# Other steps for the scales' transposes, the staged w_o rows and the memory updates of a two-layer attention and gated-MLP kernel

## The chip, the cores and the metric

The kernel runs on one core of a Trainium2 chip. The metric is the device time of one execution in microseconds (us). The engines are TensorE (PE: matmul, and PEld: its weight loads), VectorE (DVE), ScalarE (ACT), GpSimd (POOL) and SyncE (SP), whose queue issues the DMAs.

## The reference, cut to what matters

Two kinds of layer alternate twice: x + A(layernorm(x)), then x + B(layernorm(x)). x has 2048 rows of 640. A is attention with 32 heads of 20 columns in four segments of 512 rows. Inside a segment it is causal softmax attention; beside it every head reads a memory M (20 x 20) and z (20) of the segments before, and adds its own keys and values to them:

```python
for s in range(N):
    qs, ks, vs = q[:, :, s], k[:, :, s], v[:, :, s]
    p = _softmax(einsum("bhqd,bhkd->bhqk", qs, ks) * scale + mask)
    a_dot = einsum("bhqk,bhkd->bhqd", p, vs)
    num = einsum("bhld,bhde->bhle", phi(qs), M)
    den = einsum("bhld,bhd->bhl", phi(qs), z)[..., None] + 1e-6
    outs.append(g * num / den + (1.0 - g) * a_dot)
    M = M + einsum("bhld,bhle->bhde", phi(ks), vs)
    z = z + einsum("bhld->bhd", phi(ks))
```

The heads' outputs are multiplied by w_o. B is a gated MLP: z = gelu(x w_in), its second half is normalised and mixed over the 2048 rows by w_sp, multiplied with the first half, and multiplied by w_out.

## The kernel before, in words

Each of the two layers has three phases in the trace: attention (`phase1a`), the w_in products (`phase1b`), and the mixing and w_out products (`phase2`). Nearly all products are made from pairs of 16-bit halves, a high half (`h`) and a low half (`l`, what the high half leaves), after scaling by powers of two, so that an operand is always prepared by a cast on ScalarE and a subtraction on VectorE or GpSimd.

**The calendar of attention.** 64 pairs of heads (four segments, 16 pairs each) pass through a loop over steps t, from -16 up (`run`). Two pairs take five steps. A step emits, in this order: fetches of queries and keys of a later pair (`fetch`, SP), the combination of a finished pair (`combine`, VectorE and GpSimd), the logits by queries of a later pair with the maxima of their rows (`by_queries`, tile `mp`, reduced by VectorE into `mxs`), the logits by keys of the present pair (`by_keys`, tile `es`) with their exponentials (ScalarE, into `P` or `Pb`), in steps t = 5n + 2 the transposed maxima (`maxes`), whatever was posted for this step (`later`), the products of P with the values (`pvs`, tile `pv`, 20 matmuls a head), the casts of P to halves (`cast`: `PH` by ScalarE, `PL` by GpSimd, in four pieces a pair), and then the streams that are spread over the steps: layernorms of later rows, projections to q, k, v (`unit`, `value`) and by w_o (`project`), memory reads (`read`), the background weights (`background`). Work posted into `half` comes between two turns of the streams. The order of TensorE's instructions in this phase is the order in which they are emitted. The other engines' orders are chosen by the framework's scheduler from a timeline that it estimates and from priorities; `issue_after(e)` holds an instruction of e's engine behind e, and `behind(engine)` does that for the maxima and exponentials of the present step (`lead`).

**The bank "ms".** Four things share one PSUM bank (pool `apm`, tag "ms", one buffer): the transposed maxima (`mtp`, L1331, evicted by ScalarE L1333 and VectorE L1335 into `mr`, then four DMAs into the query tile, L1338), the memory update (`mup`, L1203 to L1205, 12 matmuls, evicted by VectorE L1209 into `mst`, to which GpSimd adds the old memory, L1211), the memory reads (`num`, L1175 and L1179, evicted by VectorE L1184 and L1188), and the transposes that find the weights' scales (`wtp`, L60, and `wbc`, L67).

**Updates.** A key projection's eviction (`out`) makes the feature phi(k) in one step's second half and `keys` in the next: ScalarE and VectorE split it (L1147, L1148), a transposing DMA turns it into `pk` (L1151, one buffer), and `update` is posted for the first step at least three ahead whose t mod 5 is in `UPD` and that neither is nor follows a step with a memory read. There are 15 updates a layer. Reads stand in the steps 40 s + (-6, -1, 9, 14, 24) and, for the last group of heads, 29, for segments s = 1 to 3.

**Background, layer 1 only.** Layer 1 finds the scales of w_o, w_in and w_out (`other_scales`: 32 loads into staging tiles and reductions of them, then the two transposes of `pow2_parts`), splits w_o (five rows, `Weight.behind`, L155, L81, L82) and the second half of w_in (ten pieces), and stores the halves (L166). Layer 2 loads the stored halves. The staging rows of w_o are parts of the tile that later holds the halves of w_in.

**The end of the phase.** The last half of the last pair's `PL` is made by VectorE instead of GpSimd (`TAIL`). `phase1b` begins with `load(0)` (L359, from DRAM) and the layernorm of its first row block, emitted under a raised priority, so that they mix with the end of attention; the five w_in row loads of its first half (L129) have a priority raised further, behind the last maxima's DMAs.

## Time and profile before

| | us |
|---|---|
| median of 3 runs | 2235.47 (2233.04 to 2241.97) |
| the profiled execution | 2232.87 |
| its span | 2231.2 |
| attention, layer 1 | about 27 to 603 |
| w_in products, layer 1 | about 603 to 849 |
| mixing and w_out, layer 1 | about 849 to 1133 |
| attention, layer 2 | about 1133 to 1694 |
| w_in products, layer 2 | about 1694 to 1932 |
| mixing and w_out, layer 2 | about 1932 to 2231 |

A view of groups or of waits names the waiting instruction, then the one that released it ("PE mup L1203 <- DVE mr L1335"): the total, the number of times, the longest. In a view of a queue in order of time the first two numbers are start and length, and a bracket gives the engine's idle time just before and what ended it. A view of stretches gives the length, then each engine's busy time with its number of instructions, TensorE's granted clock as a share of full speed, the DMA engines' share and GB/s. Step numbers are counted from the order in which the logits by queries (`mp`, L1249) begin: step 34 of layer 1 begins at 184.65 us, step 50 at 257.16, step 73 at 335.64; in layer 2 they begin at 1300.75, 1359.51 and 1429.37.

### The profile page before, as it was taken

To read this page: it belongs to the slowest core of one execution; us is meant where nothing else is said; L and a number is where in the kernel's file an instruction comes from. 1 tells how busy PE (TensorE), PEld (TensorE's weight loads), DVE (VectorE), ACT (ScalarE), POOL (GpSimd) and SP (SyncE) were. 2 spreads that over 40 slices of the span, in tenths; PEclk is the share of its full clock that TensorE was granted. 3 is DMA by queue.
4 is the path that set the end of the run, shared out by engine and by line. 5 is a ranking of instruction groups with operands and counts; after the bars stand their busy time and mean duration, and the time that the engine had idled before them with its cause. 6 is when DMAs were issued, how large, how long until landed. Compare 5 with 4: busy or idle time off the path is not lost.

```text
span 2231.2 us, 53044 instructions
## 1 busy us (share of the span) xinstructions
PE 2092.0 (94%) x21322; PEld 1264.7 (57%) x21322; DVE 1624.2 (73%) x2889; ACT 1252.3 (56%) x1641; POOL 1404.3 (63%) x1172
## 2 busy tenths in 40 slices
PE   6898788999899999999998999989999999999999
PEld 3554555666555555555554556656675555555555
DVE  8788778788677758888746787787875765676563
ACT  4587688788644433333325887878884433333331
POOL 3387888888645446466513888988895533564660
PEclk9999899999999999999999999999999999999999
DMA  6665556444676686676455356552456345877752
GB/s 185 157 177 141 157 150 188 109 120 126 166 195 188 180 260 191 155 189 175 132 170 129 98 128 166 127 129 75 125 137 152 98 123 175 216 181 177 166 150 83
DMA packets 537703, 342.79 MB, mean 154 GB/s; under 512 B 411600, under 2 KB 463312, under 8 KB 537456
## 3 DMA queue, kind: packets, MB, share of 16 engines
q1 hardware_dynamic: 537456, 339.39, 56.8%
q8 instruction: 167, 2.74, 0.5%
q14 instruction: 80, 0.66, 0.1%
HBM read 159.18 MB, written 92.55 MB: 113 GB/s over the span
## 4 chain that ended last, share of the span: by engine, by line
PE 67%; DVE 14%; ACT 7%; DMA 5%; issue 4%; POOL 2%; SPq 1%; DVEq 0%; ACTq 0%; POOLq 0%
PE zp L412 12%; PE ga L669 12%; PE cyp L705 7%; PE pv L1353 4%; PE qps L1110 3%; PE mp L1249 3%; PE gb L669 3%; PE vps L1051 3%; PE yps L1083 3%; PE gc L669 3%; PE gd L669 3%; DVE mxs L1313 3%; PE kps L1110 2%; PE es L1249 2%; ACT PH L1322 2%
## 5 line engine op out<-in xcount | busy, mean ns | idle before, releaser
L1324 POOL TENSOR_TENSOR PL<-P,PH 128x640 f16<-128x640 f32 x384 | 539.4, 1433 | 91.8 <-PE pv L1353 74.2
L1313 DVE TENSOR_REDUCE mxs<-mp 128x2 f32<-128x1024 f32 (+2 forms) x384 | 320.6, 862 | 135.3 <-PE mp L1240 133.7
L1287 ACT ACTIVATE P<-es,sc 128x1024 f32<-128x1024 f32 (+1 forms) x256 | 271.3, 1060 | 97.0 <-PE es L1240 92.3
L639 POOL TENSOR_TENSOR ts<-ts,wt 128x512 f32<-128x512 f32 x196 | 281.8, 1449 | 11.0
L412 PEld LDWEIGHTS <-th 128*128 128x128 f16 x1920 | 188.0, 98 | 169.3 <-issue 6.6
L1322 ACT CAST PH<-P 128x1280 f16<-128x1280 f32 x192 | 239.6, 1248 | 2.5 <-PE pv L1353 1.0
L669 PEld LDWEIGHTS <-wts 128*128 128x128 f16 x1536 | 150.7, 98 | 134.6 <-issue 6.7
L669 PE MATMUL ga<-zh,wts 128*128 128x432 f16 x768 | 212.0, 348 | 3.9 <-ACT u L736 3.9
L308 POOL TENSOR_TENSOR lnrs<-lnve,mhalf 128x1 f32<-128x1 f32 x96 | 59.7, 629 | 230.0 <-DVE lnve L307 223.7
L1324 POOL TENSOR_TENSOR PL<-Pb,PH 128x640 f16<-128x640 f32 x124 | 176.8, 1454 | 19.8 <-PE pv L1353 18.6
L412 PE MATMUL zp<-wi,th 128*128 128x432 f16 x960 | 181.2, 346 | 3.6 <-ACT z L448 3.6
L1051 PE MATMUL vps<-wvh,xt 128*128 128x320 f16 x640 | 155.5, 309 | 30.3 <-DVE relu L1142 22.1
L639 POOL TENSOR_TENSOR ts<-wt,wt 128x512 f32<-128x512 f16 x28 | 34.4, 1230 | 227.7 <-DMA wt<-wn 227.7
L669 PEld LDWEIGHTS <-wt 128*128 128x128 f16 x1152 | 112.7, 98 | 96.5
L1353 PE MATMUL pv<-vs,PH 128*128 128x41 f16 x2560 | 159.5, 183 | 8.2 <-DVE gm L1374 5.9
L705 PE MATMUL cyp<-wuh,ut 128*128 128x320 f16 (+1 forms) x896 | 163.6, 299 | 2.6 <-DMA ut<-un 1.8
L705 PEld LDWEIGHTS <-ut 128*128 128x128 f16 (+1 forms) x1344 | 131.1, 98 | 57.4 <-DMA ut<-un 3.9
L1249 PEld LDWEIGHTS <-qk 64*128 64x128 f16 (+1 forms) x2048 | 77.6, 94 | 149.4 <-issue 130.9
L1353 PE MATMUL pv<-vs,PL 128*128 128x41 f16 x2560 | 157.2, 182 | 2.2 <-POOL PL L1324 2.2
L412 PE MATMUL zp<-wi1h,th 128*128 128x432 f16 x640 | 149.8, 349 | 1.9 <-DMA th<-xnhl 1.9
L1353 PEld LDWEIGHTS <-PH 128*128 128x128 f16 x2560 | 139.4, 96 | 15.8 <-issue 5.9
L523 DVE SCALAR_TENSOR_TENSOR wn<-wr,wsc,wn 128x512 f16<-128x512 f32 x126 | 92.2, 770 | 75.5 <-ACT wn L522 75.4
(224 smaller groups left out, 5283.3 us busy)
## 6 DMA issues: line engine op xcount, KB each, us to landing
qk<-st SPq DMA_DIRECT2D x256, 120.0 KB
wr<-in_B_w_sp_dram SPq DMA_DIRECT2D x60, 512.0 KB
z<-z SPq DMA_DIRECT2D x32, 432.0 KB
cz<-z SPq DMA_DIRECT2D x32, 432.0 KB
xt<-in_A_x_dram SPq DMA_DIRECT2D x32, 320.0 KB
st<-qhl SPq DMA_DIRECT2D x40, 256.0 KB
st<-khl SPq DMA_DIRECT2D x40, 256.0 KB
x<-x SPq DMA_DIRECT2D x32, 320.0 KB
```

Source lines behind the costliest of these rows:

```text
L412: nc.tensor.matmul(zp[:, n, :FHH], a[:, k, :], b[:, k, c:c + FHH], start=(k == 0 and j == 0), stop=(k == KD - 1 and j == 2))
L639: nc.gpsimd.tensor_tensor(t, a, t if b == "t" else get(b), ALU.add if op == "+" else ALU.subtract)
L669: nc.tensor.matmul(ps, w[:, a, k % 4, :], z[:, k, j, :], start=start and k == 0 and i == 0, stop=k == NP - 1 and i == 2, skip_group_check= ...
L705: nc.tensor.matmul(yp[:, n, :320], a[:kn[k], k, :], b[:kn[k], k, n * 320:(n + 1) * 320], start=(k == 0 and j == 0), stop=(k == KO - 1 and ...
L1051: nc.tensor.matmul(ps, a[:, k, c], b[:, k, n * 320:(n + 1) * 320], start=(i == 0), stop=(i == 14))
L1110: nc.tensor.matmul(ps, a[:, k, c], b[:, k, :], start=(i == 0), stop=(i == 14))
L1249: nc.tensor.matmul(out[:, h, o:o + w], a[r, ac], b[r, bc], start=o == 0, stop=False, skip_group_check=True)
L1287: g.exp = nc.scalar.activation(P, E, AF.Exp, scale=g.esc)
L1313: e = nc.vector.tensor_reduce(mx[:, :, n, j], mp[:, :, o:o + w], AX.X, ALU.max)
L1322: nc.scalar.copy(PH, P[:, h])
L1324: (nc.gpsimd if h == 0 or n < self.N - self.TAIL else nc.vector).tensor_tensor(PL[:, c], P[:, h, c], PH[:, c], ALU.subtract)
L1353: nc.tensor.matmul(pv[:, i, h, :41], x[:, c:c + 128], v[:, j, h0 + h, :], start=(j == 0 and x is PH), stop=(j == i and x is PL), skip_grou ...
```

## The change

Six edits. `load(0)` gets three times the priority offset. `UPD` loses 2, so that no update falls into a step with the transposed maxima; `keys` is put off by a step while an update is still waiting. The last pair's low half on VectorE is posted two steps later. In the background of layer 1 the two transposes of the scales move from steps 39 and 40 to 41 and 45, the five w_o rows are loaded in steps 42 to 44 instead of 45.5 to 47.5 and split from step 47 instead of 48; and every step of the weights' work is also held behind the exponentials of its step on ScalarE.

```diff
@@ phase1b
+        with tc.high_priority(offset=3 * HP2):
+            a = load(0)
         with tc.high_priority(offset=HP2):
-            a = load(0)
             xn = attn_out(0, *a)
@@
-UPD = (2, 3, 4, 0)
+UPD = (3, 4, 0)
@@ Attention.__init__
-        self.mem, self.last, self.stacked = False, -1, -1
+        self.mem, self.last, self.stacked, self.waiting = False, -1, -1, False
@@ Attention.out
         def keys(ph):
+            if self.waiting:
+                self.post(1, lambda: keys(ph))
+                return
+            self.waiting = True
             hl = self.u3.tile([128, 2, L], F16, tag="hl", name="phl")
@@ Attention.update
         assert self.pk_of == (s, m), (self.pk_of, s, m)
+        self.waiting = False
@@ Attention.cast
-        for c in (slice(0, 640), slice(640, 1280))[::-1 if n % 2 and h else 1]:
-            (nc.gpsimd if h == 0 or n < self.N - self.TAIL else nc.vector).tensor_tensor(PL[:, c], P[:, h, c], PH[:, c], ALU.subtract)
+
+        def low(engine):
+            for c in (slice(0, 640), slice(640, 1280))[::-1 if n % 2 and h else 1]:
+                engine.tensor_tensor(PL[:, c], P[:, h, c], PH[:, c], ALU.subtract)
+
+        if h == 0 or n < self.N - self.TAIL:
+            low(nc.gpsimd)
+        else:
+            self.post(2, lambda: low(nc.vector))
@@ Attention.run, background
             if not made:
-                for i, _ in enumerate(other_scales(g, self.place, self.pl1, self.pm, "ms")):
+                scales = other_scales(g, self.place, self.pl1, self.pm, "ms")
+                for i, more in enumerate(scales):
+                    if not more:
+                        break
                     yield 5 + i
-            yield 45
-            yield 45.5
-            for j, (w, width) in enumerate(((g.wo, D), (g.wi[1], FHH))):
-                w.tiles(g.top[j])
...
-                else:
-                    parts = [...]
-                    it = w.behind(lambda _: next(rows), width, KD)
-                    times = [46 + i / 2 for i in range(KD)] + [49 + 1.4 * i for i in range(99)]
-                for i in range(99):
-                    with self.tc.issue_after(self.fetched.ins):
-                        if next(it, it) is it:
-                            break
-                    yield times[i]
+                yield 41
+                next(scales)
+
+            def steps(it, times):
+                for t in times:
+                    with self.tc.issue_after(self.fetched.ins), self.behind(ACT):
                         if next(it, it) is it:
                             break
+                    yield t
+
+            g.wo.tiles(g.top[0])
+            if made:
+                yield 45.5
+                yield from steps(g.wo.load(self.bg, D, "bg"), [46 + 1.4 * i for i in range(99)])
+                g.wi[1].tiles(g.top[1])
+                yield from steps(g.wi[1].load(self.bg, FHH, "bg"), [54 + 1.4 * i for i in range(99)])
+            else:
+                parts = [...]
+                rows = iter([parts[k // 3][:, k % 3] for k in range(KD)])
+                it = g.wo.behind(lambda _: next(rows), D, KD)
+                yield 42
+                yield from steps(it, [42.5, 43, 43.5, 44, 45])
+                next(scales, None)
+                yield 47
+                yield from steps(it, [48.4 + 1.4 * i for i in range(99)])
+                g.wi[1].tiles(g.top[1])
+                yield from steps(g.wi[1].behind(self.place, FHH, 2), [56 + 1.9 * i for i in range(99)])
```

## The prediction

> **What bounds it now.** I read the page first, then the busy time of stretches, then who waited for whom in the stretches where the two layers differ, then single queues in order of time.

> ```profile
> span 2231.2 us, 53044 instructions
> PE 2092.0 (94%) x21322; PEld 1264.7 (57%) x21322; DVE 1624.2 (73%) x2889; ACT 1252.3 (56%) x1641; POOL 1404.3 (63%) x1172
> PE 67%; DVE 14%; ACT 7%; DMA 5%; issue 4%; POOL 2%; SPq 1%; DVEq 0%; ACTq 0%; POOLq 0%
> ```

> TensorE carries the kernel: busy 94%, and two thirds of the chain that ended last. The change takes no matmul away, so it can only win where TensorE waits. The edits lie in the attention phases (about 27 to 603 and 1133 to 1694 us), and there the two layers are a comparison: they do the same attention, but only layer 1 finds scales and splits w_o and the second half of w_in beside it. The busy times of steps 34 to 49 and 50 to 72, layer 1 first (columns: length, busy time of each engine with its instructions, granted clock, DMA):

> ```profile
> 184.65:257.16 72.51, 53.22 (x754) 34.56 (x754) 53.87 (x105) 51.26 (x65) 53.88 (x48) 0.90 0.55 148
> 257.16:335.64 78.48, 69.10 (x1049) 44.91 (x1049) 61.42 (x104) 61.24 (x78) 65.63 (x59) 0.98 0.49 143
> 1300.75:1359.51 58.76, 51.36 (x751) 33.42 (x751) 47.03 (x89) 47.08 (x60) 53.81 (x50) 0.97 0.67 159
> 1359.51:1429.37 69.86, 68.19 (x1049) 44.31 (x1050) 50.58 (x95) 56.95 (x69) 61.43 (x58) 0.98 0.53 131
> ```

> The same matmuls take 13.75 us longer in steps 34 to 49 of layer 1 (72.51 - 58.76), at a lower clock, and 8.62 us longer in steps 50 to 72.

> **Scales and w_o rows (layer 1 alone).** The waits of 184 to 257 us (total, times, longest), and after them those of 1300 to 1360 us:

> ```profile
> PE vps L1051 <- DVE relu L1142: 8.8, 1, 8.8
> DVE relu L1142 <- ACT kps L1137: 7.2, 2, 6.6
> ...
> ACT woh L81 <- DMA wsth<-in_A_wo_dram: 4.1, 1, 4.1
> ...
> PE wbc L67 <- DVE gm L1188: 3.5, 1, 3.5
> ...
> PE wtp L60 <- DVE lnmv L306: 2.7, 1, 2.7
> ```
> ```profile
> PE vps L1051 <- DVE relu L1142: 2.7, 1, 2.7
> ...
> PE num L1175 <- DVE lnmv L306: 1.5, 1, 1.5
> ```
> ```profile
> 229.85 0.41 SPq L155 DMA_DIRECT2D wsth<-in_A_wo_dram  x1
> ...
> 233.06 0.83 ACT L81 ACTIVATE woh<-wsth,iv 128x640 f16<-128x640 f32 x1 [4.13 <-DMA wsth<-in_A_wo_dram]
> ...
> 236.51 0.66 ACT L1137 ACTIVATE kps<-kps,sc 128x512 f32<-128x512 f32 x1
> ```

> Read from the bottom: ScalarE ran the first w_o split in step 44, four steps ahead of the step that emits it, and stood 4.13 us for its row. Behind it in the same queue was the exponential of kps; VectorE's relu waits for that, and TensorE's vps for the bank that relu frees: 8.8 us, against 2.7 in layer 2. The scales' two transposes share the one "ms" bank with memory reads: in step 39 wtp waits 2.7 us for the last update's eviction (layer 2's read waits 1.5 there anyway), in step 40 wbc waits 3.5 for the read of step 39. Net of layer 2 these are 6.1 + 1.2 + 3.5 = 10.8 of the 13.75 us; the rest is mostly clock and added work.

> The change puts wtp into step 41 and wbc into step 45, after the read of 39 and the update of 43 have been evicted, asks for the five rows in steps 42 to 44, and holds each split behind the exponentials of its own step, the first in step 47. A row took 3.2 us from issue to use (229.85 to 233.06) and now has three steps of about 4.5 us (72.51 / 16). What stays is work: VectorE is busy 53.87 - 47.03 = 6.84 us longer in this stretch. If nothing covers that, 6.9 of the 13.75 come back; if all is covered, 13.75. VectorE is idle a quarter of the stretch, so I count about half, 4 us with the transposes themselves: **-9.75**. Two new costs can lower it. Step 42's transposed maxima now take the bank from wtp, so their matmul waits for a VectorE reduce, and the casts' products, projections and step 43's logits queue behind it: bounded by wtp's 2.7. The five rows pass SP's queue ahead of maxima rows and query/key fetches; those of step 42 are first needed in step 45, so I count zero, at worst the row's 3.2. Range -13.75 to -1.

> **w_in splits.** The same hold applies to the ten w_in pieces of layer 1 (waits of 257 to 336 us):

> ```profile
> ACT wi1h L81 <- DMA wst<-in_B_w_in_dram: 7.4, 5, 3.2
> ```

> ScalarE stood 7.4 us here with exponentials behind it. The excess of this stretch is 8.62, but VectorE has 61.42 - 50.58 = 10.84 us of added work in it, which stays; I leave 6 of the 8.62: **-2.6**, range -7.4 to 0. In layer 2 the weights are only reloaded by the same DMAs at the same steps: nothing.

> **Updates out of the maxima's step (both layers).** Who waited for the maxima's bank, and what memory reads wait for:

> ```profile
>   PE mup L1203: 12.9, 9
> ```
> ```profile
>   DVE mst L1209: 4.9, 6
> ```

> Five updates a layer share step 5n+2 with the transposed maxima (12, 67, 82, 87, 92 by the calendar in the code); their 12 matmuls wait until VectorE has evicted the maxima: 12.9 us in all. They move one step on (13, 68, 83, 88, 93), with their eviction and GpSimd's addition. By site, where the waits were, and how long VectorE itself then starved:

> ```profile
> PE mup L1203 <- DVE mr L1335: 1.7, 1, 1.7
> ```
> ```profile
> PE mup L1203 <- DVE mr L1335: 4.9, 3, 2.3
> ```
> ```profile
> PE mup L1203 <- DVE mr L1335: 5.2, 3, 2.4
> ```
> ```profile
> 371.62 1.29 DVE L1313 TENSOR_REDUCE mxs<-mp 128x2 f32<-128x768 f32 x2 [0.62 <-PE mp L1240]
> ...
> 408.51 1.29 DVE L1313 TENSOR_REDUCE mxs<-mp 128x2 f32<-128x768 f32 x2 [2.35 <-PE mp L1240]
> ```

> The rows are step 12 of layer 1, then steps 82 to 92 of either layer. After step 92's wait VectorE starved 2.35 us, so that wait is on the path; after step 82's only 0.62, VectorE being the late engine there. I count 0.62 for step 82's 1.96 in each layer: 12.9 - 2.7 = 10.2 us won. Against it, the updates of 68, 88 and 93 now stand one step ahead of the reads of 69, 89 and 94, which take the same bank from them. Six reads stand so already, and waited 4.9 us: 0.82 each. Six more cost 4.9; behind such a read stand the next step's logits, and VectorE's maxima and ScalarE's exponentials wait for those. Two features a layer (steps 83 and 88) slip a step: one ScalarE and one VectorE instruction and a transposing DMA in another order, with three steps until the update; I count zero, bounded either way by one VectorE pass such as the 1.29 us above. Net -5.3.

> The clock adds to it. TensorE, busy (nearly) throughout, ran at half the granted clock (0.50) after the waits of step 92:

> ```profile
> 406.70:410.10 3.40, 3.40 (x60) 2.59 (x59) 1.59 (x3) 1.67 (x3) 0.00 (x0) 0.50 0.99 105
> 1498.90:1502.30 3.40, 3.08 (x31) 2.27 (x31) 0.71 (x2) 1.42 (x2) 0.43 (x1) 0.51 0.54 119
> ```

> Half of 3.4 us is lost each time; with VectorE partly late I count 1 each: **-7.3** in all, range -12.9 - 3.4 = -16 to 0 (each new read wait at the 2.7 of wtp: 6 x 2.7 = 16 eats the gain).

> [...]

> **The end of attention.** load(0) of the next phase is put three times as far ahead; the last low half moves behind a combine (570 to 604 us, then 1663 to 1695):

> ```profile
> DVE lnst L305 <- DMA x<-x: 3.9, 1, 3.9
> ...
> ACT xn L391 <- DVE neg L390: 3.1, 1, 3.1
> PE pv L1353 <- DVE gm L1374: 2.9, 1, 2.9
> ...
> POOL lnrs L308 <- DVE neg L390: 2.1, 1, 2.1
> ```
> ```profile
> DVE lnst L305 <- DMA x<-x: 4.2, 1, 4.2
> ...
> POOL PL L1324 <- PE pv L1353: 1.3, 1, 1.3
> ```
> ```profile
> 577.52 1.82 SPq L129 DMA_DIRECT2D wst<-in_B_w_in_dram  x4
> 579.39 0.49 SPq L1075 DMA_DIRECT2D xt<-in_A_x_dram  x1
> 579.92 0.43 SPq L359 DMA_DIRECT2D x<-x  x1
> ```

> The row x1 is asked for behind four w_in rows; the next phase's statistics stand in VectorE's queue for it, and ScalarE and GpSimd behind them, while the last pairs are unfinished. SP shows no wait of its own, so an earlier place is free. What is late next is GpSimd's low halves: I count its idle, 2.1 and 1.3. The last low half:

> ```profile
> 596.38 3.11 DVE L1324 TENSOR_TENSOR PL<-Pb,PH 128x640 f16<-128x640 f32 x2
> ...
> 600.96 0.31 DVE L1374 TENSOR_TENSOR gm<-pv,gm 128x160 f32<-128x160 f32 x1
> ```
> ```profile
> 601.41 1.56 PE pv L1353 x40
> ```

> Now it lies ahead of gm, for which all 40 products wait; after, the first 20 need only gm and run beside it: half of 1.56, 0.8 a layer, up to 1.7 if the projections' evictions slip behind too; I take 1. Together 2.1 + 1.3 + 2 = **-5.4**, range -11.5 (3.9 + 4.2 + 3.4) to +1.5 (one more late eviction).

> **Sum.** -9.75 - 2.6 - 7.3 - 5.4 = -25 us. The profiled execution took 2232.87 us (span 2231.2), 2.6 under the median of 2235.47; so 2208 against it, 2210.5 against the median.

> **Rivals.** *All of layer 1's excess goes*: 13.75 + 8.62 instead of 12.35, -35, 2200.5. For it, in steps 34 to 49 both layers' TensorE is equally busy; against, VectorE's added work stays. *The waits come back at the reads*, because VectorE, not TensorE, is late from step 82 on: updates give nothing and half of step 41's and 45's gain goes to VectorE's queue: -25 + 7.3 + 5 = -12.7, 2223. The 0.62 of step 82 speaks for it, the 2.35 of step 92 against. *It does not do what it says*: VectorE, ScalarE, GpSimd and SP are ordered by the scheduler's own estimate, as the split run four steps early shows; if x1 still stands behind the w_in rows and vps still waits for the old reasons, 5.4 + 6.1 + 2.6 go: -11, 2224.5. *Slower*: held splits that find their row missing now block ScalarE with exponentials behind. All fifteen waiting as the six seen did, (4.1 + 7.4)/6 = 1.9 each, is 28.8 against 11.5 now; with the first two parts' gains gone it is +17.3 - 7.3 - 5.4 = +4.6; at the longest seen, 5 x 4.1 + 10 x 3.2 = 52.5, it is +28. So 2240 to 2264, about 2250, decided where a row lands later than its step's exponential. Against: rows have three steps, and landed within 3.2 us.

> **How the numbers follow.** Chances: forecast 0.50, all of the excess 0.14, back at the reads 0.16, orders kept 0.12, slower 0.08. A change under 0.5% (11.2 us) can't be told from none here, so faster means under 2224.3. Of the third case half falls on either side, of the fourth nearly all in "same", of the last some. Faster 0.72, same 0.21, slower 0.07. The range 2198 to 2228 leaves out the slow case, half of the fastest and a little of the forecast.

> **What would show it.** Right: no TensorE wait over 3 us in steps 39 to 45 of layer 1, that stretch near 62 us; no wait of w_o splits for a row; mup never waiting for mr, num waiting for mst twelve times and about 10 us; lnst without a wait for x<-x in the last steps; no half-speed window after step 92. Wrong: num or the maxima's transposes taking over the 12.9 us, ScalarE waiting at L81 for rows, or the stretch of layer 1 still over 70 us.

## The result and the profile after

The changed kernel takes 2221.95 us (median of 7, 2218.56 to 2225.51), the kernel before 2233.04 on the same chip (7, 2228.73 to 2241.97): ratio 0.9948, 95% interval 0.993 to 0.9965. The forecast was 2210.5 in a range of 2198 to 2228. Direction and range held; of the 25 us of the sum some 11 came (2233.04 - 2221.95). The page of the kernel after, in the lines shown of before:

```profile
span 2220.2 us, 53079 instructions
PE 2084.5 (94%) x21322; PEld 1261.3 (57%) x21322; DVE 1622.2 (73%) x2889; ACT 1251.7 (56%) x1641; POOL 1402.9 (63%) x1172
PE 67%; DVE 14%; ACT 7%; DMA 4%; issue 4%; POOL 3%; SPq 1%; ACTq 0%; DVEq 0%; POOLq 0%
```

The span is 11.0 us shorter (2231.2 - 2220.2), and 7.5 us of that are TensorE's busy time, though it does the same matmuls: the trace of before has 16 windows of 3.41 us in which the granted clock is 0.50, that of after has 9 (the one at the very end not counted), and the mean granted clock rose from 0.987 to 0.993. Only 3.5 us are less idle time. So part of what a shorter wait gives comes through the clock. The stretches tell where. First steps 34 to 49, 50 to 72 and 87 to 90 of layer 1 and 87 to 90 of layer 2 after, then 87 to 90 of both layers before:

```profile
186.94:252.41 65.47, 51.62 (x755) 33.76 (x755) 53.14 (x106) 49.89 (x63) 53.39 (x48) 0.95 0.59 154
252.41:325.50 73.09, 67.38 (x1051) 43.93 (x1050) 60.99 (x105) 62.43 (x79) 66.01 (x60) 1.00 0.55 161
...
372.14:391.69 19.55, 14.87 (x202) 10.68 (x203) 14.05 (x29) 12.41 (x17) 15.11 (x14) 0.91 0.58 148
1464.04:1483.64 19.60, 14.91 (x201) 10.75 (x201) 14.06 (x29) 12.40 (x17) 15.40 (x14) 0.91 0.55 132
```
```profile
384.07:398.84 14.77, 14.13 (x203) 10.27 (x203) 12.67 (x24) 12.80 (x18) 13.92 (x13) 0.93 0.70 189
1477.09:1491.74 14.65, 13.88 (x202) 10.34 (x201) 12.34 (x23) 12.60 (x17) 13.51 (x12) 0.95 0.70 174
```

The background stretches of layer 1 won 7.0 us (72.51 to 65.47) and 5.4 us (78.48 to 73.09). Steps 79 to 86 won 2.2 and 2.5 us in the two layers and steps 91 to 96 2.4 and 2.5 (differences of step starts), but steps 87 to 90, between them, lost 4.8 and 4.95. The end of attention, from step 151 to the first product of the next phase (`zp`), changed by +0.05 and -1.1; the -1.1 is there without the edits at the end too (29.94 us in run e1 below, 29.96 here, 31.08 before, which has two half-speed windows there). So the moved updates gave and took the same amount, and the gain is layer 1's background work.

What became of the maxima's bank: who waits for `mr`, then what memory reads wait for, then the waits of 184 to 252 us:

```profile
who waited for it (us, times):
  DVE mr L1348: 3.1, 11
```
```profile
  DVE lnmv L306: 8.3, 4
...
  PE num L1180: 5.7, 8
```
```profile
PE vps L1052 <- DVE relu L1143: 5.0, 1, 5.0
...
DVE relu L1143 <- ACT kps L1138: 3.5, 3, 2.6
...
PE wtp L60 <- DVE gm L1193: 2.3, 1, 2.3
```

No `mup` waits for `mr` any more (12.9 us before), and the reads wait 14.0 us (8.3 + 5.7). Here is VectorE's queue at the read of step 89, and then the read on TensorE:

```profile
382.05 1.23 DVE L1316 TENSOR_REDUCE mxs<-mp 128x4 f32<-128x1024 f32 x1 [2.07 <-PE mp L1246]
383.19 0.88 DVE L305 BATCH_NORM_STATS2 lnst<-xt 128x6 f32<-128x320 f32 x2
383.98 0.73 DVE L1153 SCALAR_TENSOR_TENSOR phl<-relu,sc,phl 128x512 f16<-128x512 f32 x1
384.64 0.48 DVE L1058 SCALAR_TENSOR_TENSOR vs<-vps,vs 128x320 f16<-128x320 f32 x1
385.04 0.32 DVE L1215 TENSOR_TENSOR mst<-mup,bmask 128x168 f32<-128x168 f32 x1
...
388.18 1.23 DVE L1319 TENSOR_REDUCE mxs<-mp 128x2 f32<-128x1024 f32 x1 [2.52 <-PE mp L1246]
```
```profile
385.51 0.46 PE L1180 MATMUL num<-mst,phq 128*128 128x126 f32 x2 [2.65 <-DVE lnmv L306]
```

The update's eviction takes 0.32 us but is fifth in the queue, behind a layernorm's statistics, the feature that the change put off into this very step (`phl`), and a value's eviction. The read behind it waits 2.65 us (the view names `lnmv`, which ran beside the eviction's end); the logits behind the read come late, and VectorE, which was idle for 2.1 us in all of these four steps before (14.77 - 12.67), starves for 2.52 us, as it had for 2.07 us just before, in step 88. Of the 4.8 us, 2.9 lie in step 89 and 1.4 in step 90, which stands under a half-speed window. In the step that it left, 87, this update had made TensorE wait much less (before, layer 1, then layer 2):

```profile
PE mup L1203 <- DVE mr L1335: 0.6, 1, 0.6
```
```profile
PE mup L1203 <- DVE mr L1335: 0.8, 1, 0.8
```

### The profile page after: what moved, and what is told of

Read it like the earlier page. It is cut to its first block, busy times and chain, and to the rows that moved or that the text cites. A ratio compares the mean times of both kernels' runs of the same rounds, so it can differ in the third digit from the quotient of the medians.

```text
span 2220.2 us, 53079 instructions
## 1 busy us (share of the span) xinstructions
PE 2084.5 (94%) x21322; PEld 1261.3 (57%) x21322; DVE 1622.2 (73%) x2889; ACT 1251.7 (56%) x1641; POOL 1402.9 (63%) x1172
## 4 chain that ended last, share of the span: by engine, by line
PE 67%; DVE 14%; ACT 7%; DMA 4%; issue 4%; POOL 3%; SPq 1%; ACTq 0%; DVEq 0%; POOLq 0%
PE zp L412 13%; PE ga L670 12%; PE cyp L706 7%; PE pv L1366 4%; PE qps L1111 4%; PE gb L670 3%; PE mp L1255 3%; PE yps L1084 3%; DVE mxs L1319 3%; PE vps L1052 3%; PE gc L670 3%; PE gd L670 3%; PE kps L1111 2%; PE es L1255 2%; ACT PH L1328 2%
## 5 line engine op out<-in xcount | busy, mean ns | idle before, releaser
L308 POOL TENSOR_TENSOR lnrs<-lnve,mhalf 128x1 f32<-128x1 f32 x96 | 59.8, 631 | 233.5 <-DVE lnve L307 226.8
```

## The experiments

The kernels ran on three chips, in fours, each four beside the kernel before: its medians were 2233.51 (first four), 2233.7 (next four) and 2233.27 us (last four). A length of steps is the difference of two step starts, and lengths and waits are those of one profiled execution of each kernel.

| run | median us | ratio to before, interval |
|---|---|---|
| e1_background_only | 2221.35 | 0.9943, 0.993 to 0.9956 |
| e2_updates_only | 2232.78 | 1.0003, 0.9991 to 1.0015 |
| e3_end_only | 2231.93 | 1.0, 0.9989 to 1.001 |
| e4_update_87_kept | 2209.98 | 0.9896, 0.9883 to 0.9909 |
| e5_eviction_first | 2208.26 | 0.9884, 0.9863 to 0.9906 |
| e6_hold_only | 2228.35 | 0.9963, 0.9948 to 0.9978 |
| e7_block_8_early | 2218.32 | 0.9921, 0.99 to 0.9941 |
| e8_low_half_behind | 2208.98 | 0.9888, 0.9865 to 0.991 |
| e9_keep_and_first | 2207.71 | 0.9889, 0.9871 to 0.9907 |
| e10_first_old_steps | 2213.47 | 0.9913, 0.9897 to 0.9929 |
| e11_first_and_low | 2204.04 | 0.9865, 0.9844 to 0.9886 |
| e12_steps_without_hold | 2225.36 | 0.9965, 0.9953 to 0.9977 |

The theory after the result: the background edit made the whole gain; the updates' waits came back at the reads because the eviction stands late in VectorE's queue; the two edits at the end of attention reached neither the row nor the order they meant. Rivals: the updates helped, and the clock or the end took it back; or the background edit gave more and all else cost.

### One part alone

e1 is the kernel before with only the last hunk of the diff (`background`).

> The kernel before with the background's edit alone (scales' transposes, w_o rows, splits held behind the exponentials). Theory A, read from the two traces: this part makes the whole gain, 11 to 12 us (steps 34 to 73 of layer 1 about 12.4 us shorter), ratio about 0.995. Theory B, the forecast's terms with a loss elsewhere: also about 12 us. Theory C, it needs the moved updates beside it: 5 us or less.

e2 has only the moved updates:

```diff
-UPD = (2, 3, 4, 0)
+UPD = (3, 4, 0)
...
+            if self.waiting:
+                self.post(1, lambda: keys(ph))
+                return
+            self.waiting = True
```

> The kernel before with the moved updates and the put-off features alone. Theory A: what steps 12, 67, 82, 87 and 92 win is paid back in steps 87 to 91 (4.8 us a layer more), so 0 to 1 us faster, ratio 0.9995 to 1.0; no wait of the update for the maxima, reads waiting about 14 us in all. Theory B, the forecast: 7 us faster, ratio 0.997.

e3 has only the priority of `load(0)` and the low half posted two steps later:

```diff
+        with tc.high_priority(offset=3 * HP2):
+            a = load(0)
...
+            self.post(2, lambda: low(nc.vector))
```

> The kernel before with the raised priority of load(0) and the later low half alone. Theory A: nothing moves, since load(0) went out some 50 us before the end of attention already and the row that VectorE stands for is row block 8; ratio 1.000 within 0.001. Theory B, the forecast: 5 us faster, ratio 0.9976.

e1 alone gives the changed kernel's time, e2 and e3 nothing that can be told from none. In e2 steps 87 to 90 took 3.4 and 8.0 us longer than before, steps 79 to 86 and 91 to 96 of both layers 2.2 to 2.5 shorter each. The move from step 67 to 68 made steps 67 to 72 shorter by 0.9 us in layer 1 and longer by 1.0 in layer 2.

### The read of step 89

e4 is the changed kernel with one of the moved updates, that of step 87, back in its old step (the feature that was put off behind it, from step 88 to 89, goes back with it):

```diff
+KEEP = (87,)
...
-        while c is not None and (t % 5 not in c or t in self.rd or t - 1 in self.rd):
+        while c is not None and (t % 5 not in c and t not in KEEP or t in self.rd or t - 1 in self.rd):
```

> The changed kernel, but the one update of step 87 stays there instead of moving to step 88, right ahead of the read of step 89. Theory A, the read right behind the moved update pays (2.65 us of wait, the late step 90, the half-speed window): steps 87 to 91 go back from 19.6 to about 14.7 us in each layer, 9 to 10 us faster than the changed kernel, about 2212. Rival D, VectorE is late there whatever TensorE does, and the wait only changes its name: under 3 us.

e5 leaves the updates where the change put them and queues their eviction ahead of the other work posted to that step:

```diff
-        self.post(1, out)
+        if self.now is None:
+            out()
+        else:
+            self.later.setdefault(self.now + 1, []).insert(0, out)
```

> The changed kernel, with the update's eviction posted ahead of everything else of its step, so that VectorE does it right behind the maxima; step 88 keeps its update. Theory A1: the read of step 89 waits 2.65 us because in VectorE's queue the eviction stands behind row statistics (0.88), the put-off feature (0.73) and a value eviction (0.48); with these 2 us behind it the wait falls to about 0.6, and reads wait 14 us no more but 5 to 7 in all: 5 to 9 us faster than the changed kernel, about 2215. Rival A2: VectorE reaches that step late anyway and the time comes back at the next wait for it: within 2 us of the changed kernel.

Steps 87 to 90 of both layers in e4:

```profile
369.67:385.27 15.60, 13.22 (x202) 9.98 (x203) 14.04 (x28) 12.30 (x17) 14.38 (x13) 1.00 0.71 187
1455.07:1470.68 15.61, 13.22 (x201) 9.98 (x203) 14.05 (x28) 12.29 (x17) 14.40 (x13) 1.00 0.60 163
```

They are 4 us shorter than in the changed kernel, at full clock, though `mup` waits 4.8 us for `mr` again (two times). VectorE's queue and the read of step 89 in e5:

```profile
377.31 1.23 DVE L1319 TENSOR_REDUCE mxs<-mp 128x4 f32<-128x1024 f32 x1 [3.69 <-PE mp L1249]
378.45 0.32 DVE L1215 TENSOR_TENSOR mst<-mup,bmask 128x168 f32<-128x168 f32 x1
```
```profile
378.92 0.46 PE L1180 MATMUL num<-mst,phq 128*128 128x126 f32 x2 [0.80 <-DVE mst L1215]
```

The eviction is now second, and the read waits 0.80 us instead of 2.65. In all, the reads wait 5.5 us in e5 instead of 14.0. That shows the queue to be the cause of the wait. Both kernels gained more than expected, 12 and about 14 us against the changed kernel. In e4, 7.9 of the span's 11.9 lie in these two stretches and 3.0 in steps 8 to 33 of layer 1, which the edit leaves alone (last section). In e5 steps 8 to 33 of layer 1 are shorter by the same 3.0, though e4 has that without the new order, and steps 87 to 90 by only 1.4 and 2.1: at 18.18 and 17.46 us they are still longer than before, with a half-speed window in step 88 of each layer (372.54 and 1457.97 us) in place of the one behind the read. The same eviction order also shortened steps 34 to 49: 62.39 us against 65.47 in layer 1 and 56.40 against 57.99 in layer 2.

### The two halves of the background edit

e6 is the kernel before with the hold alone, e12 the background edit without it:

```diff
-                    with self.tc.issue_after(self.fetched.ins):
+                    with self.tc.issue_after(self.fetched.ins), self.behind(ACT):
```

> The kernel before, with one thing of the background's edit alone: its steps are also held behind the exponentials on ScalarE; transposes and w_o rows stay at their old steps. Theory A: the hold makes two thirds of the background's 12 us, since ScalarE no longer stands for rows (4.1 and 7.4 us): 7 to 9 us faster, ratio about 0.9965, with wtp and wbc still waiting 2.7 and 3.5 us. Rival: the transposes' new steps make most of it, and the hold gives 3 us or less.

> The kernel before with the scales' transposes and the w_o rows at their new steps, but splits not held behind their step's exponentials: the part of the background edit that the run with the hold alone did not have. If the two parts add up to the whole (12 us, the hold 5 to 8 of it), 2226 to 2229 us, with the 8.8 us wait of vps gone since a row has landed when its split runs early. Rival, without the hold the scheduler again runs a split ahead of its row: vps still waits over 7 us and the time stays at 2231 to 2235 us.

The waits of steps 34 to 49 of layer 1 in e6, then of steps 34 to 72 in e12:

```profile
PE vps L1051 <- DVE relu L1142: 4.9, 1, 4.9
...
PE wbc L67 <- DVE gm L1188: 3.5, 1, 3.5
```
```profile
PE vps L1051 <- DVE relu L1142: 4.9, 1, 4.9
ACT wi1h L81 <- DMA wst<-in_B_w_in_dram: 4.8, 4, 2.0
```

Either half alone takes `vps` from 8.8 to 4.9 us: held splits stand behind the exponential, and early rows have landed when a split runs early. Only the new steps remove the wait of `wbc`, only the hold those of the w_in splits. The gains add: 2.6 and 3.9 us in steps 34 to 49 (7.1 in e1), 3.3 and 1.4 in steps 50 to 72 (4.4 in e1), and by medians 5 and 8 against 12 us. The sums are rough: by the ratios it is 8 and 8 against 13, and e6's twelve runs spread from 2217.99 to 2230.96 us. Of e12's 1.4 us, 1.1 are step 50 (4.02 to 2.90 us), most of which a half-speed window had covered before (from 256.49 us).

### The end of attention

e7 is e4 with row block 8, the second in `phase1b`'s order, loaded at the raised priority too. e8 is e4 with the low half bound behind the combine:

```diff
-            a = load(0)
+            a, b = load(0), load(ORDER[1])
```
```diff
-            self.post(2, lambda: low(nc.vector))
+            def late():
+                with self.tc.issue_after(self.joined.ins):
+                    low(nc.vector)
+            self.post(2, late)
...
-            nc.vector.tensor_tensor(o, a, o, ALU.add)
+            self.joined = nc.vector.tensor_tensor(o, a, o, ALU.add)
```

> As the changed kernel with the update of step 87 kept, and the load of row block 8 raised with that of block 0, which puts it ahead of the four w_in rows in SP's queue. The forecast's mechanism at the right row: VectorE's wait for x (4.3 and 4.0 us) goes or falls under 1.5 us, and the end of attention (step 145 to the first zp) is 2 us shorter in layer 1 and 1 in layer 2, about 2207 in all. Rival: GpSimd's low halves and the last products set the end anyway, and only the wait goes: under 0.7 us in all.

> As the changed kernel with the update of step 87 kept, and the last low half held behind gm on VectorE, which posting it two steps later did not do. The forecast's mechanism: the first 20 products run beside the low half, 0.8 to 1.7 us a layer off the end of attention. Rival: the low half now ends later by the work put ahead of it, and the last products wait as long: within 0.5 us a layer.

e7 took VectorE's wait for the row from 4.6 to 2.5 us in layer 1, but the end of attention became only 0.95 us shorter there and 1.7 longer in layer 2: in layer 1 the scheduler answered the earlier load by putting that block's statistics one combine earlier in VectorE's queue, and in layer 2, where they kept their place, a half-speed window that e4 doesn't have stands in that stretch (from 1658.61 us). The other 7 us by which its span exceeds e4's lie elsewhere, 3.1 of them in steps 8 to 33 of layer 1, ahead of the edit. All of the excess shows as clock: TensorE is busy 9.0 us longer than in e4 and idle 0.9 us less, with 11 half-speed windows against 5. So e7's time doesn't tell what the earlier row is worth.

e8 shortened layer 1's end by 2.7 us and lengthened layer 2's by 1.3, and the time is that of e4. The clock hides the edit here too: e4 has a half-speed window in the end of layer 1 (from 578.33 us), e8 in that of layer 2 (from 1654.39). From the start of VectorE's last combine but one to the first product of the next phase, behind these windows, e4 takes 5.8 and 5.7 us and e8 4.2 in either layer, with `gm` ahead of the low half in both.

### Together

e9 is e4 with e5's eviction. e10 is e1 with e5's eviction: every update in its old step. e11 is e9 with e8's bound low half.

> The changed kernel with the update of step 87 kept in its step and the update's eviction ahead of the other posted work of its step: both earlier gains at once. If they come from two places (the read of step 89, and VectorE's queue in steps 34 to 50 and at the other reads), steps 87 to 91 take about 15.5 us and steps 34 to 50 about 62.4 and 56.4 us, and the time is 2204 to 2206 us, 4 to 6 under the kernel with the step kept. Rival, both are the same wait at the read of step 89, and the rest was the clock: 2208 to 2211 us.

> The kernel before with the new background work and the eviction first, but with every update in its old step and no feature put off. If the moves of the updates are worth what steps 79 to 87 and 91 to 97 showed (2.2 + 2.4 and 2.5 + 2.5 us, 9.6 in all), it stands 8 to 10 us above the run with eviction first and step 87 kept: 2213 to 2216 us. Rival, the eviction's place alone does it, since the updates' own waits lie under VectorE's lateness: 2204 to 2208 us, and then the first idea of moving updates was worth nothing.

> As the run with step 87 kept and the eviction first, and the last low half of a layer bound behind the combine. With step 87 kept alone, the bound low half made the end of layer 1 shorter by 2.7 us and that of layer 2 longer by 1.3, and the time the same. Expected 1 to 2 us under the run without it, 2203 to 2205 us; rival, no difference.

Steps 34 to 49 of layer 1 and 87 to 90 of both layers in e9:

```profile
184.03:246.39 62.36, 53.90 (x755) 34.95 (x755) 53.25 (x106) 49.59 (x63) 53.24 (x48) 0.92 0.66 161
...
366.28:380.78 14.50, 13.22 (x203) 9.98 (x203) 12.53 (x28) 12.57 (x17) 14.50 (x13) 1.00 0.77 189
1451.90:1466.41 14.51, 13.23 (x203) 9.99 (x203) 12.66 (x28) 12.64 (x17) 14.51 (x13) 1.00 0.84 175
```

The stretches of e9 are what the two-places idea expected, 87 to 90 even a microsecond shorter. Its median, 2207.71, lies between the two ideas (2204 to 2206, 2208 to 2211) and cannot be told from e5's; 2.6 us more than in e5 stand in the mixing phase of layer 1, which no edit touches, with a half-speed window there (from 830.83 us). e10 differs from e1 by the eviction's place alone, and that is worth 7 to 8 us (ratios 0.9943 and 0.9913, medians 2221.35 and 2213.47, on two chips), although no update moved. e10 also came out where the first idea put it, 2213 to 2216, though nearer to e9 than the 8 to 10 us expected: with the eviction first, moving the updates (but that of step 87) is worth 5.8 us (2213.47 - 2207.71; e9 also has the two edits at the end, which gave nothing in e3). In e10 `mup` still waits 14.6 us for `mr`. So the moves were no bad idea; they lacked the place in VectorE's queue. e11 has the lowest median of this study, 29 us under before, though its interval overlaps that of e9. The ends of attention in e9, then in e11, where the order of the low half at last is the one that the change meant:

```profile
549.98:583.55 33.57, 25.18 (x421) 18.18 (x421) 15.67 (x43) 21.36 (x23) 25.69 (x20) 0.97 0.84 189
...
1635.61:1665.38 29.77, 24.62 (x422) 17.77 (x422) 15.43 (x43) 21.47 (x23) 25.14 (x20) 1.00 0.52 150
```
```profile
553.92:584.91 30.99, 26.10 (x422) 18.58 (x421) 14.61 (x43) 20.52 (x22) 25.09 (x20) 0.94 0.83 194
1638.03:1666.31 28.28, 24.56 (x421) 17.90 (x421) 14.92 (x43) 21.46 (x23) 25.11 (x20) 1.00 0.56 151
```
```profile
582.49 0.33 DVE L1395 TENSOR_TENSOR gm<-pv,gm 128x160 f32<-128x160 f32 x1
582.73 1.60 DVE L1336 TENSOR_TENSOR PL<-Pb,PH 128x640 f16<-128x640 f32 x2
```

2.6 and 1.5 us, 4.1 together, against 3.7 by the medians. In layer 2 both stretches ran at full clock, and in layer 1 e11 had the lower clock, so this is the order and not the clock.

## Why the prediction was right and wrong, step by step

The time fell into the range, but two of the four parts gave nothing, and the two that gave came to their forecast sum (12.35; 7.0 + 5.4 = 12.4) because one was too large and the other too small: that is luck as much as reading. The premise that the change "can only win where TensorE waits" was too narrow. The sum had 2 us for the clock, while TensorE's busy time fell by 7.5 us and its idle time by 3.5.

**Scales and w_o rows** (-9.75; 7.0 came). The mechanism was right: no w_o split waits for its row, the wait of `wbc` is gone, and `vps` waits less. Two sizes were off. The prediction had `wtp` in step 41 find the bank free, "after the read of 39 and the update of 43 have been evicted" (the update of 43 concerns `wbc`); it still waits 2.3 us for that read (2.7 before), because the step between, without its transpose, shrank from 6.5 to 1.9 us. And `vps` was to fall from 8.8 to layer 2's 2.7 but stays at 5.0, though no split waits for a row: its exponential is late for another reason. With the eviction first that stretch is 62.36 us, near the 62 of the forecast, and in e9 `wtp` waits 1.1 and `vps` 2.9 us: much of both had waited on the same VectorE queue.

**w_in splits** (-2.6; 5.4). Held splits wait for no row, and what their removal was worth was underrated: 4.4 us in e1, of which 1.1 are the half-speed window that left step 50. Another 1.0 belong to the update moved from 67 to 68 (steps 67 to 72 take 20.2 us, 21.2 in e1).

**Updates** (-7.3; 0). The waits removed were counted right in sum, 12.9 us to none, and steps 79 to 86 and 91 to 96 won 2.2 to 2.5 us each in either layer; but the three sites of "steps 82 to 92" were taken as alike, and step 87 had only 0.6 and 0.8 us to win. The step that failed is "Six more cost 4.9": the reads wait 7.6 us more (14.0 against 4.9 + 1.5), and the wait of step 89 alone, with VectorE's lateness and a half-speed window behind it, cost 4.8 and 4.95 us of path. The put-off feature, for which "I count zero", is one of the three instructions ahead of the eviction. The rival that the waits come back at the reads, at 0.16, is what happened to this part, and its 2223 us was nearer than the forecast; its nearness is in part luck, though, since it let half of step 41's and 45's gain go, kept 5.4 us for the end, which gave none, and had 2.6 for the w_in splits.

**The end** (-5.4; 0 in e3). Both steps failed, and on reading the trace of before more closely they could have been seen to. The row "asked for behind four w_in rows" is not `load(0)`: that one left SP's queue some 60 us earlier, in the kernel before (first row) as after (second), and the awaited one (third, after) is row block 8, whose rows a late projection stores.

```profile
520.86 0.35 SPq L359 DMA_DIRECT2D x<-x  x1
```
```profile
511.23 0.35 SPq L359 DMA_DIRECT2D x<-x  x1
...
568.34 1.86 SPq L129 DMA_DIRECT2D wst<-in_B_w_in_dram  x4
...
570.73 0.44 SPq L359 DMA_DIRECT2D x<-x  x1
```

A low half emitted two steps later is still ahead of `gm` in VectorE's queue after the change, since the scheduler chooses that order:

```profile
587.83 2.77 DVE L1332 TENSOR_TENSOR PL<-Pb,PH 128x640 f16<-128x640 f32 x2
...
591.67 0.31 DVE L1387 TENSOR_TENSOR gm<-pv,gm 128x160 f32<-128x160 f32 x1
```

The rival "does not do what it says" was right for this part alone. The price of the low half, 1 us a layer, was under what e11 gained with the order bound (2.6 and 1.5).

**Signs.** Of the five, "mup never waiting for mr" and the w_o rows came; TensorE still waited over 3 us in step 44 (`vps`, 5.0), and that stretch took 65.47 and not 62; the reads waited 14.0 and not about 10; the row's wait stayed (4.3 us); the half-speed windows after step 92 went, and came back after the read of step 89.

## What to carry to other kernels

A wait that was moved to another reader of the same bank became as long as the queue in front of the instruction that frees the bank: before moving, read that engine's queue at the new place, price the wait at both places (here 0.6 us at the old one and 2.65 at the new), and put the eviction first. A change of priority or of emission order is only a wish where a scheduler orders the queues; bind the order, and find in the trace which very transfer is waited for. Price each part alone: here one part made all the gain, one gave and took some 9.6 us, and one did nothing.

## What the runs showed of the hardware

```profile
103.95:107.36 3.41, 1.56 (x36) 1.17 (x33) 3.41 (x8) 3.35 (x5) 3.07 (x4) 1.00 0.56 163
107.36:110.77 3.41, 3.15 (x31) 1.78 (x31) 2.35 (x8) 0.72 (x1) 3.41 (x3) 0.50 0.80 235
383.84:387.25 3.41, 1.74 (x16) 1.77 (x16) 1.79 (x6) 1.13 (x2) 1.38 (x3) 1.00 0.70 181
387.25:390.66 3.41, 3.41 (x41) 2.13 (x40) 2.34 (x5) 1.89 (x2) 1.00 (x1) 0.50 0.03 5
```
```profile
830.91:834.33 3.42, 1.49 (x9) 0.80 (x9) 3.42 (x5) 1.47 (x3) 0.16 (x1) 1.00 0.43 103
834.33:837.74 3.41, 3.41 (x21) 1.93 (x20) 3.38 (x4) 0.00 (x0) 0.00 (x0) 1.00 0.19 43
```

So idle time in one cell, in one wait or in several (1.26 and 0.37 us ahead of the window of before that starts at 382.78), can cost the next cell half its clock. The longest single wait ahead of 387.25 was 2.65 us, shorter than a cell. Counted over the cells at full clock of all fourteen traces (40 to 2190 us, each on its own grid): all 77 with TensorE idle for 2.0 us or more were followed by half speed, 15 of 38 with 1.7 to 2.0 us, 24 of 403 with 1.0 to 1.7, and none with less (in before and after alone: 11 of 11, 2 of 5, 7 of 60, none of 1159). What decides between 1.0 and 2.0 us is open.

The place on the grid seems to be worth a few microseconds by itself. e4 and e7 have the same instructions in the same order on every engine up to step 145 of layer 1; their steps 8 to 33 of layer 1, e4 first:

```profile
103.05:184.27 81.22, 72.92 (x1173) 44.38 (x1173) 72.98 (x135) 72.67 (x91) 69.36 (x59) 1.00 0.67 183
```
```profile
100.72:185.04 84.32, 76.06 (x1172) 45.64 (x1171) 73.54 (x135) 72.64 (x91) 69.26 (x59) 0.96 0.67 176
```

3.1 us, at 1.00 and 0.96 of the clock. The changed kernel, with the same work in these steps, takes 84.16 us at 0.96: a cell begins 1.17 us behind the start of its step 8, has 1.85 us idle, and half speed follows. In e4 the cell begins 0.83 us behind that start, has 1.51 us idle, and full speed follows. That the place decides is my reading; no run sets it. Each row is one profiled execution, and the timed runs of one kernel do not share one clock: e7's shortest took 2211.53 us at a mean granted clock of 0.995, its longest 2219.22 at 0.991; e6's 2217.99 at 0.995 and 2230.96 at 0.989. So differences of 2 to 4 us between e4, e5, e8 and e9 can be the clock alone, and which of them is best is not settled.
